# A sliding-window branch beside full attention: V copied into shifted partition groups and summed by a selection matrix, with a new layout table

## The chip, the cores and the metric

The kernel runs on one core of a Trainium2 chip. The metric is the time of one execution on the device in microseconds. Three runs of the kernel before took 825.7, 826.05 and 822.5 us: the median is 825.7.

## The reference

Two attention layers read the same x (2048 tokens, 640 features, 32 heads of 20 features, bf16), and a gate mixes them.

```python
x = A_x
g = sigmoid((x * gate_w).sum(-1, keepdims=True))
a = A_ref(x, A_wqkv, A_wo)      # full softmax attention over 2048 keys
b = B_ref(x, B_wqkv, B_wo)      # 8 taps: key positions s, s-2, ..., s-14
return g * a + (1 - g) * b

# B_ref, after its own q, k, v projections:
W, dil = 8, 2
logits = einsum("bhsd,bhswd->bhsw", q, kg) * Dh ** -0.5   # kg, vg: k, v at the taps
logits = where(mask, logits, -1e9)                        # positions before 0
attn = softmax(logits, axis=-1)
o = einsum("bhsw,bhswd->bhsd", attn, vg)
return o.reshape(B, S, D) @ wo
```

## The kernel before, in words

**Full attention.** The 32 heads form 8 groups of 4, the 2048 queries 4 chunks of 512; a pair of both is one of 32 groups of work, each with 16 key blocks of 128 and 4 heads: 64 blocks of 128 keys x 512 queries. PE computes scores (line 1568, four heads in four row groups of the array), then one of two engines takes the exponential. ACT does most blocks, in tiles of two or three (line 1592, `ebuf`). A block may instead "ride" in the third place of a tile and go to DVE: line 1582 turns the score into a 16-bit integer whose bits are a coarse exponential (`uD`), line 850 makes three shifted copies per four blocks (`eD`), and PE adds four weighted products (line 1637) where a block from ACT needs one. `obank` collects a group; `gen_norm` transposes, divides by the row sums, applies the gate and copies the result into `oTd` by DMA.

**Sliding branch.** It works in 8 units `u` of 256 tokens, with features on partitions in the order 32 * a + head, five chunks f, so a feature is the pair (a, f). `gen_bproj(u)` projects q, k, v into `qkvB` (`qB`, `kB`, `vB`; the last two with 16 columns of the unit before, copied by POOL at line 893). `gen_b(u)` then

1. multiplies q by k shifted, one DVE product of 128x1280 for each of the 8 taps (line 922, into `stage`);
2. sums them over features with the selection matrix `Sel` (line 938): partition 32 * w4 + head then holds the logits of tap w4, with the taps' upper half beside it in the free dimension;
3. takes the maximum over taps on DVE (lines 952 to 960), subtracts it by a matmul (line 964), and lets ACT write `eB` (line 967);
4. copies each tap's 32 rows of `eB` to all four partition groups by four DMAs of 32 KB (`taps`, line 972) into one of three buffers `repB`;
5. computes the row sums and the gate (lines 985 to 1006) and spreads them by DMA into `rB`;
6. multiplies v shifted by the copied tap, again 8 products of 128x1280 (line 1023), once `fold` of the chunk before has freed `oB`;
7. sums the 8 products with identity matmuls (line 610, through `mm_group`): 8 taps for each of three banks, each as four column tiles, and writes `oB` (line 1040).

`gen_fold` multiplies `oB` and `oTd` by the output weights and stores 128 rows at a time. For the last chunk this is done early in part: `gen_prefold` (two row blocks, then, as the third step, the last 128 columns of all four), `gen_prefold2` (the other two row blocks), and `tail` adds what the very last group of heads contributes.

**What sets the order.** All engines run lists in order, with semaphores between them. A planner writes the lists: it goes through the ACT tiles, numbered s, and between them lets generators issue side work on PE and DVE where its own clock says that there is room. Each generator has a priority (the units 5.6, their projections 6.5, prefold 2.2 and so on). `bank` lends one of three PSUM banks (one of its own, the two score tiles' third place). `PLAN` is a table: at certain s it sets 18 knobs, among them how idle DVE must look before blocks ride, how far ahead DVE may be filled, and how full PE must be before filler matmuls (line 1658) are put in. The lines of the change: 50 to 137 (`PLAN`), 489 and 492 (first weights through `repB`), 889 (V's projection waits for the products of the unit before), 914 to 1045 (`gen_b`), 1053 to 1085 (`fold_mms`, `gen_prefold`).

Of the kernel before, what the change touches and what calls it, by code (L numbers as in the profile page):

```python
# [14 lines left out]
P = 128  # L15
# [357 lines left out]
def _build(ctx, nc, A_x, A_wqkv, A_wo, B_wqkv, B_wo, gate_w, out):  # L373
# [16 lines left out]


    NE = 5
    NR = 3
    NV0 = 1
    xT = sb([P, CN, S], BF16, "xT")
    WqP = sb([P, CN, P], BF16, "WqP")
    kvw = sb([P, 3 * CN * D], BF16, "kvw")
    woA_d = sb([P, CN, D], BF16, "woA_d")
    woBp = sb([P, CN, D], BF16, "woBp")
    kT = sb([P, NQ, S], BF16, "kT")  # L400
# [511 lines left out]
    def gen_b(u):  # L912
# [62 lines left out]
        for i in range(NR):  # L975
            taps(i)
# [855 lines left out]
```

## Time and profile before

| | |
|---|---|
| median of three runs | 825.7 us |
| profiled execution, span from first to last instruction | 821.3 us |
| ACT, PE, DVE, POOL busy | 784.6, 771.7, 718.2, 148.0 us |
| ACT tiles of two and of three blocks | 474 and 245 |
| blocks on DVE | 364 |
| products of the sliding branch on DVE | 128, 104.3 us |
| DMA packets | 45014, 29.12 MB |

The profile gives the profiled execution's span and no other time of it; the runs' median stands 4.4 us above the span. PE is an engine for matmuls, PEld its weight loads, DVE the vector engine, ACT the one that does exponentials, POOL a second vector engine, SP the queue that issues nearly all DMAs. In a row of the groups the columns are line, engine, operation, output<-input by the program's names, shapes, count, then busy time in us, mean ns of one, idle time before them and what ended it. In a row of the timeline the columns are start and duration in us, engine, line, operation and count; a row can merge several instructions.

### The profile page before, as it was taken

The page shows a single profiled execution, that of the slowest core. Times are in us where ns is not written, and L with a number is a line of the kernel's source. Part 1 is how long each engine was busy: PE and PEld are TensorE (multiplying, and loading weights), DVE is VectorE, ACT ScalarE, POOL GpSimd, SP SyncE. Part 2 cuts the span into 40 slices and gives each one's busy share as a digit, 9 for nine tenths or more (in the row PEclk, how much of TensorE's full clock was granted, in tenths as well). Part 3 has the DMA queues.
Part 4 walks back from the last instruction along what each step waited for, and adds up shares of the span by engine and source line. Part 5 has one row for each costly group of instructions (what it writes and reads, how often), then busy time and mean ns, then how long its engine had stood idle before and what let it go on. Part 6 is the DMA issues. An engine that isn't in the chain of part 4 may idle for free.

```text
span 821.3 us, 29318 instructions
## 1 busy us (share of the span) xinstructions
PE 771.7 (94%) x12399; PEld 280.8 (34%) x12401; DVE 718.2 (87%) x1261; ACT 784.6 (96%) x752; POOL 148.0 (18%) x204
## 2 busy tenths in 40 slices
PE   8999999989899999999999999999998998989997
PEld 5332223333333332434234332333333323343333
DVE  7587899589998998997899999999899998998973
ACT  4999999999999999999999999999999999999990
POOL 5013114151111111010111021131211121111010
PEclk9999999999999999999999999999999999999999
DMA  9110222100111011011001110010010110110010
GB/s 310 39 36 22 54 45 62 41 15 16 32 31 40 8 43 23 7 44 31 19 6 35 39 37 21 28 32 21 5 30 13 36 21 13 27 33 5 23 41 34
DMA packets 45014, 29.12 MB, mean 35 GB/s; under 512 B 27204, under 2 KB 43684, under 8 KB 44884
## 3 DMA queue, kind: packets, MB, share of 16 engines
q1 hardware_dynamic: 44596, 26.92, 12.6%
q8 instruction: 98, 1.61, 0.8%
q10 hardware_dynamic: 288, 0.33, 0.1%
q14 instruction: 32, 0.26, 0.1%
HBM read 11.94 MB, written 2.62 MB: 18 GB/s over the span
## 4 chain that ended last, share of the span: by engine, by line
PE 37%; ACT 31%; DVE 17%; issue 14%; POOL 0%; ACTq 0%; DVEq 0%
ACT ebuf L1592 30%; PE score L1568 11%; PE obank L1637 9%; PE side L610 9%; DVE uD L1582 7%; DVE eD L850 4%; PE score L610 4%; PE obank L1658 1%; DVE qkvB L906 1%; DVE stage L1023 1%; PE obank L512 1%; DVE stage L922 1%; PE score L1283 1%; ACT eB L967 0%; DVE oB L1040 0%
## 5 line engine op out<-in xcount | busy, mean ns | idle before, releaser
L1592 ACT ACTIVATE ebuf<-score 128x1024 bf16<-128x1024 f32 (+1 forms) x720 | 773.2, 1245 | 9.2 <-PE score L1568 7.7
L1568 PE MATMUL score<-qT,kT 32*128 32x512 bf16 x2048 | 285.0, 385 | 29.2 <-ACT ebuf L1592 18.6
L1582 DVE TENSOR_SCALAR uD<-score 128x512 int16<-128x512 f32 x364 | 240.4, 678 | 20.6 <-PE score L1568 19.3
L850 DVE TENSOR_SCALAR eD<-uD 128x2048 int16<-128x2048 int16 x273 | 192.9, 729 | 2.5 <-PE obank L1637 1.7
L1568 PEld LDWEIGHTS score<-qT,kT 32*128 32x128 bf16 x2048 | 70.8, 91 | 267.4 <-ACT ebuf L1592 186.5
L1637 PE MATMUL obank<-ebuf,vA 128*21 128x512 bf16 x1684 | 156.8, 386 | 1.9 <-DVE eD L850 0.5
L842 POOL TENSOR_TENSOR vS<-vA,vw 128x252 bf16<-128x252 bf16 x91 | 66.7, 735 | 278.6 <-PE obank L1637 246.5
L610 PE MATMUL side<-xT,kvw 128*32 128x256 bf16 (+1 forms) x2550 | 105.9, 282 | 2.4 <-DVE qkvB L906 1.4
L1637 PE MATMUL obank<-eD,vS 128*21 128x512 bf16 x1092 | 95.9, 380 | 0.0
L610 PEld LDWEIGHTS side<-xT,kvw 128*32 128x32 bf16 x2550 | 58.3, 96 | 39.9 <-issue 17.7
L1637 PEld LDWEIGHTS obank<-ebuf,vA 128*21 128x21 bf16 x1684 | 36.9, 89 | 86.1 <-issue 61.4
L817 POOL TENSOR_TENSOR rcp<-rcp,gA 128x16 f32<-128x16 f32 x31 | 9.7, 313 | 306.2 <-DVE rcp L815 306.2
L1023 DVE TENSOR_TENSOR stage<-qkvB,repB 128x1280 bf16<-128x1280 bf16 x64 | 52.7, 844 | 0.1
L922 DVE TENSOR_TENSOR stage<-qkvB 128x1280 bf16<-128x1280 bf16 x64 | 51.6, 834 | 0.1
L906 DVE CAST qkvB<-side 128x512 bf16<-128x512 f32 (+1 forms) x71 | 41.2, 589 | 5.5 <-PE side L610 5.2
L610 PE MATMUL side<-stage,ident 128*32 128x512 bf16 (+1 forms) x704 | 44.7, 348 | 1.0 <-DVE dst L714 0.5
L1637 PE MATMUL obank<-uD,vA 128*21 128x512 bf16 x364 | 35.3, 379 | 0.0
L823 POOL TENSOR_TENSOR oN<-oTt,rcp 128x512 bf16<-128x512 f32 x31 | 33.3, 1074 | 2.4
L1637 PEld LDWEIGHTS obank<-eD,vS 128*21 128x21 bf16 x1092 | 26.8, 92 | 17.2 <-issue 1.4
L811 DVE STREAM_TRANSPOSE oTt<-obank 128x512 f32<-128x512 f32 x32 | 22.7, 709 | 5.2 <-PE obank L1637 4.9
L610 PE MATMUL side<-woA_d,oTd 128*32 128x512 bf16 (+2 forms) x500 | 26.7, 304 | 0.0
L610 PE MATMUL side<-woBp,oB 128*32 128x512 bf16 (+1 forms) x500 | 24.9, 304 | 1.0 <-DVE qkvB L906 0.6
(172 smaller groups left out, 534.9 us busy)
## 6 DMA issues: line engine op xcount, KB each, us to landing
repB<-eB SPq DMA_DIRECT2D x128, 32.0 KB
WqP<-in_A_wqkv_dram SPq DMA_DIRECT2D x16, 160.0 KB
stage<-in_B_wqkv_dram SPq DMA_DIRECT2D x1, 2400.0 KB
oTd<-oN SPq DMA_DIRECT2D x108, 20.0 KB
qT<-dst SPq DMA_DIRECT2D x104, 20.0 KB
out_dram<-outsb SPq DMA_DIRECT2D x12, 160.0 KB
kvw<-in_A_wqkv_dram SPq DMA_DIRECT2D x2, 800.0 KB
oTd<-in_A_x_dram SPq DMA_DIRECT2D x2, 640.0 KB
```

The costliest lines, as they stand in the source:

```text
L610: ins = e.matmul(o[j:k, :], l(j) if callable(l) else l[:, j:k], r, start=(first and i == 0), stop=(last and i == n - 1), skip_group_check= ...
L811: T("dve", 0.625, lambda e: e.transpose(oTt[:, :], obank[:, :]), reads=["obank"], writes=["oTt"])
L823: T(en, c2, lambda e: e.tensor_tensor(oo, ii, ib, ALU.mult), reads=["rcp", "oTt"], writes=["oN0"])
L842: T("pool", 0.607, lambda e: e.tensor_tensor(vS[:, d % 2, :, :], _ap(vA, (kb * NQ + q) * 4 * DV, [[0, K - 1], [1, 4 * DV]]), _ap(vw, 0, [[ ...
L850: T("dve", 0.065 + 0.1334 * n, lambda e, k=k, sl=sl: e.tensor_scalar(eD[:, sl % NS, 0:512 * n].bitcast(I16), uD[d % 2][:, 0:512 * n].bitca ...
L906: t = TB(dvc(n * TOK), lambda e, o=o, i=i: e.tensor_copy(o, i), reads=[("side", b)], writes=[key])
L922: TB(dvc(CN * TOK, 2), lambda e, w=w, ks=ks: e.tensor_tensor(prodB(w), qB[:, :, :], ks, ALU.mult), reads=["qB", "kB"], writes=[("prod", w) ...
L1023: TB(dvc(CN * TOK, 2), lambda e, w=w, vs=vs, rr=rr: e.tensor_tensor(prodB(w), vs, rr, ALU.mult), reads=["vB", ("repB", w4 % NR)], writes=[ ...
L1568: ins = e.matmul(o, kT[32 * j:32 * j + 32, q, kb * P:(kb + 1) * P], qT[g % NQT][32 * j:32 * j + 32, :], start=True, stop=True)
L1582: t = T("dve", 0.598, lambda e: e.tensor_scalar(uD[d % 2][:, 512 * i:512 * (i + 1)].bitcast(I16), side[x], UOFF, 0.0, op0=ALU.add, op1=ALU ...
L1592: exps[s] = T("act", actc(512 * n), lambda e: e.activation(ebuf[s % NE][:, 0:512 * n], score[s % 2][:, 0:512 * n], ACTF.Exp, scale=LN2 / S ...
L1637: ins = e.matmul(obank[32 * j:32 * j + DV, :], v, src, start=(kb == 0), stop=(last and k >= len(lst) - 4), skip_group_check=True)
```

## The change

- **V instead of the taps is copied.** At the end of `gen_bproj(u)`, once the V products of the unit before are done, 16 DMAs fill `vR`, the second part of `stage`: partition group w4 gets all four 32-row groups of `vB`, shifted by 4 * w4 tokens, rows of 258 tokens. The tap copies and `repB` go; V's projection itself no longer waits for the unit before.
- **Taps are numbered anew**: tap w = 2 * w4 + hh. In `vR` partition 32 * w4 + head meets `eB` with the same partition, and the tap sum becomes a sum over partition groups, done by `Sel` with 256 columns (`v_sum`) in place of identity matmuls.
- **Products go by feature chunk**: 5 products of 128x2048 for q and k, 5 for v, in a ring of three buffers, each summed by PE as soon as it is there.
- The maximum gets buffers of its own (`mxB`) and is subtracted by a matmul over 128 rows, with zeros in `negRep` beyond row 32.
- The last chunk of the output weights, 48 rows, is loaded into a zeroed tile (`woA_z`, in the place of `WqP`), so that prefold's matmuls all have 128 rows.
- The first weights go through `ebuf[3]` and `ebuf[4]`.
- `PLAN` has other entries throughout.

```diff
 PLAN = {
-    0: ((0.3, 0.64), 0.31, 1.0, 2.5, 0.49, -1.34, -0.1, 11.8, 7.0, 6.03, 0.52, 0.47, 4.4, 4.0, 0.0, 0.71, 3, -1.5),
...
+    0: ((0.29, 0.69), 0.16, 1.0, 5.5, 0.94, -1.37, 0.17, 9.99, 7.0, 7.54, 0.6, 0.62, 5.69, 5.04, 0.0, 0.65, 2, -3),
...
-    stage = sb([P, WIN * CN * TOK], BF16, "stage")
+    CH = WIN * TOK
+    NCH = 3
+    VW = TOK + DIL
+    stage = sb([P, NCH * CH + 4 * CN * VW], BF16, "stage")
+    vR = _ap(stage, NCH * CH, [[VW, 4 * CN], [1, VW]])
...
-            while m == 2 and u > 0 and not done.get(("bp", u - 1)):
-                yield ("cond",)
...
+        while u > 0 and not done.get(("bp", u - 1)):
+            yield ("cond",)
+        for w4 in range(4):
+            lo = PADB - DIL - 2 * DIL * w4
+            T("sp", 2.0 + 0.65 * 4, lambda e, w4=w4, lo=lo: [e.dma_start(
+                vR[32 * w4:32 * w4 + 32, a * CN:(a + 1) * CN, :], vB[32 * a:32 * a + 32, :, lo:lo + VW]) for a in range(4)],
+              reads=["vB"], writes=[("vR", w4)] + (["stage"] if u == 0 else []), dma=True, nd=4, iss=0.65)
...
+        def q_chunk(f):
+            i = slot[f] = next_chunk()
+            yield ("dve", DVE_AHEAD, sch.free(("prod", i)))
+            o = _ap(stage, i * CH, [[4 * TOK, 2], [TOK, 4], [1, TOK]])
+            i0 = _ap(qkvB, f * TOK, [[0, 2], [0, 4], [1, TOK]])
+            i1 = _ap(qkvB, CN * TOK + f * (TOK + PADB) + PADB, [[-DIL, 2], [-2 * DIL, 4], [1, TOK]])
+            TB(dvc(CH, 2), lambda e: e.tensor_tensor(o, i0, i1, ALU.mult),
...
+        for f in range(NCH):
+            yield from q_chunk(f)
...
+        for f in range(CN):
+            yield from q_sum(f, b)
+            if f + NCH < CN:
+                yield from q_chunk(f + NCH)
...
-        for i in range(NR):
-            taps(i)
...
-        for w4 in range(4):
-            for hh in range(2):
-                w = 4 * hh + w4
-                yield ("dve", DVE_AHEAD, sch.ready(("repB", w4 % NR)))
...
-            if w4 + NR < 4:
-                taps(w4 + NR)
-        done[("bp", u)] = True
+        def v_chunk(f):
+            i = slot[f] = next_chunk()
+            yield ("dve", DVE_AHEAD, max(sch.free(("prod", i)), sch.ready("eB", *[("vR", w4) for w4 in range(4)], to="dve")))
+            o = _ap(stage, i * CH, [[4 * TOK, 2], [TOK, 4], [1, TOK]])
+            i0 = _ap(stage, NCH * CH + f * VW + DIL, [[-DIL, 2], [CN * VW, 4], [1, TOK]])
+            i1 = _ap(eB, 0, [[TOK, 2], [0, 4], [1, TOK]])
...
+        def v_sum(f, k, b):
...
+                    for a in range(4):
+                        ins = e.matmul(side[b][32 * a:32 * a + 32, k * TOK:(k + 1) * TOK], Sel,
+                                       _ap(stage, i * CH + (4 * hh + a) * TOK, [[1, TOK]]),
...
         for f0 in range(0, CN, 2):
             n = min(2, CN - f0)
+            for f in range(f0, f0 + n):
+                yield from v_chunk(f)
...
-            mms = [(side[b][:, 0:n * TOK], ident[:, :], _ap(stage, (w * CN + f0) * TOK, [[1, n * TOK]]))
-                   for w in (0, 4, 1, 5, 2, 6, 3, 7)]
...
+            for k in range(n):
+                yield from v_sum(f0 + k, k, b)
...
-        rows = [P] * (CN - 1) + [D - 4 * DH - (CN - 1) * P]
...
+        wl = [woA_d[:, f, c0:c1] for f in range(CN - 1)] + [woA_z[:, c0:c1]]
...
+    def gen_wz():
+        while not done.get(("q", NG - 1)):
+            yield ("cond",)
+        T("pool", 0.8, lambda e: e.memset(woA_z.bitcast(FP32), 0.0), writes=WQ)
+        rows = D - 4 * DH - (CN - 1) * P
+        T("sp", 5.0, lambda e: e.dma_start(woA_z[0:rows, :], A_wo[D - rows:D, :]), writes=WQ, dma=True)
+        done["wz"] = True
```

More of the change, by code (lines that the diff above doesn't have):

```diff
@@ L444, in _build @@
     rB = sb([P, TOK], FP32, "rB")
[L445 to L447 removed]
+    mxB = [sb([P, TOK], BF16, "mxB%d" % i) for i in range(2)]
+    mB = mxB[1][:, 0:TOK]
+    cB = mxB[0][0:64, 0:TOK]
     oB = sb([P, CN, 512], BF16, "oB")
@@ new lines, in q_sum, with fn @@
+        def q_sum(f, b):
+            rd = [("prod", slot[f]), "Rep"]
+            for hh in range(2):
+                yield ("pe", 0.11, sch.ready(*rd))
+                def fn(e, hh=hh, i=slot[f]):
+                    for w4 in range(4):
+                        ins = e.matmul(side[b][32 * w4:32 * w4 + 32, hh * TOK:(hh + 1) * TOK], Sel,
+                                       _ap(stage, i * CH + (4 * hh + w4) * TOK, [[1, TOK]]),
+                                       start=(hh == 0 and f == 0), stop=(hh == 1 and f == CN - 1), skip_group_check=True)
+                    return ins
+                T("pe", 0.11, fn, reads=rd, mode="col", **({"writes": [("side", b)]} if (hh == 0 and f == 0) else {"accum": [("side", b)]}))
@@ new lines, in v_sum, with fn @@
+        def v_sum(f, k, b):
+            rd = [("prod", slot[f]), "Rep"]
+            for hh in range(2):
+                yield ("pe", 0.11, sch.ready(*rd))
+                def fn(e, hh=hh, i=slot[f]):
+                    for a in range(4):
+                        ins = e.matmul(side[b][32 * a:32 * a + 32, k * TOK:(k + 1) * TOK], Sel,
+                                       _ap(stage, i * CH + (4 * hh + a) * TOK, [[1, TOK]]),
+                                       start=(hh == 0 and k == 0), stop=(hh == 1), skip_group_check=True)
+                    return ins
+                T("pe", 0.11, fn, reads=rd, mode="col", **({"writes": [("side", b)]} if (hh == 0 and k == 0) else {"accum": [("side", b)]}))
@@ L1070, in gen_prefold @@
                 yield ("cond",)
-            rd = [("oTd", (QCN - 1) % 2, q) for q in range(1, NQ)] + ["woA_d", "woBp"] + [
+            rd = [("oTd", (QCN - 1) % 2, q) for q in range(NQ)] + ["woA_d", "woBp"] + WQ + [
                 ("oB", hu, f0) for hu in range(1 + (i == 2)) for f0 in range(0, CN, 2)]
@@ L1096, in gen_prefold2 @@
             yield ("cond",)
-        rd = [("oTd", (QCN - 1) % 2, q) for q in range(1, NQ)] + ["woA_d", "woBp"] + [
+        rd = [("oTd", (QCN - 1) % 2, q) for q in range(NQ)] + ["woA_d", "woBp"] + WQ + [
             ("oB", hu, f0) for hu in range(2) for f0 in range(0, CN, 2)]
```

88 lines of the change are left out of this document (33 added, 55 removed), and 193 rows, old and new, of the table PLAN.

## The prediction

> **What bounds the kernel now.** I read the head of the page first, then the busy time in stretches of 75 us, then the groups of instructions kept apart by shape, and last the order of time at the end.
>
> ```profile
> span 821.3 us, 29318 instructions
> PE 771.7 (94%) x12399; PEld 280.8 (34%) x12401; DVE 718.2 (87%) x1261; ACT 784.6 (96%) x752; POOL 148.0 (18%) x204
> ...
> 325.00:400.00 75.00, 70.22 (x1256) 27.78 (x1248) 66.75 (x118) 74.81 (x71) 10.43 (x19) 1.00 0.09 24
> 475.00:550.00 75.00, 70.84 (x1172) 24.05 (x1164) 71.95 (x126) 74.56 (x74) 15.50 (x20) 1.00 0.12 30
> 800.00:821.30 21.30, 15.44 (x396) 8.01 (x391) 7.70 (x14) 2.39 (x4) 0.00 (x0) 1.00 0.09 33
> ```
>
> The columns of the stretches are PE, PEld, DVE, ACT, POOL, clock, DMA share, GB/s. Inside the run ACT is full: 74.81 of 75 us. DVE has 8.3 us to spare in its emptiest stretch and 3.1 in its fullest. Only at the end ACT is empty: 2.39 of 21.3 us. So time can come from two places: fewer tiles on ACT, which needs DVE to take them, and a shorter end.
>
> ```profile
> L1592 ACT ACTIVATE ebuf<-score 128x1024 bf16<-128x1024 f32 x474 | 458.6, 1099 | 5.5 <-PE score L1568 4.3
> L1592 ACT ACTIVATE ebuf<-score 128x1536 bf16<-128x1536 f32 x245 | 346.8, 1530 | 3.7 <-PE score L1568 3.4
> L1582 DVE TENSOR_SCALAR uD<-score 128x512 int16<-128x512 f32 x364 | 240.4, 678 | 20.6 <-PE score L1568 19.3 <-ACT g L801 0.2
> L850 DVE TENSOR_SCALAR eD<-uD 128x2048 int16<-128x2048 int16 x273 | 192.9, 729 | 2.5 <-PE obank L1637 1.7
> L1023 DVE TENSOR_TENSOR stage<-qkvB,repB 128x1280 bf16<-128x1280 bf16 x64 | 52.7, 844 | 0.1
> L922 DVE TENSOR_TENSOR stage<-qkvB 128x1280 bf16<-128x1280 bf16 x64 | 51.6, 834 | 0.1
> L957 DVE TENSOR_TENSOR repB<-repB 64x256 bf16<-64x256 bf16 x8 | 2.3, 284 | 0.3
> L938 PE MATMUL side<-stage,Rep 128*32 128x256 bf16 x320 | 13.2, 285 | 0.5 <-DVE qkvB L906 0.5
> ...
> L610 PE MATMUL side<-stage,ident 128*32 128x512 bf16 (+1 forms) x704 | 44.7, 348 | 1.0 <-DVE dst L714 0.5
> sum 796.30, PE 34.84 PEld 9.41; mean PE 2.90 PEld 0.78
> ```
>
> The exchange rate: ACT takes (458.6 + 346.8) / (2 x 474 + 3 x 245) = 0.48 us for a head's 128x512 block, DVE (240.4 + 192.9) / 364 = 1.19 us. To end d earlier, ACT must hand over d / 0.48 blocks, so DVE works 2.5 d more in d less time: DVE time freed is worth 1 / 3.5 of itself. The last row is the filler matmuls of line 1658 alone, 34.84 us: PE has that much time without real work, so freeing PE by itself buys little in mid-run.
>
> **The change part by part.** *Products.* 16 of 128x1280 per unit of 256 tokens cost (52.7 + 51.6) / 8 = 13.04 us of DVE. They become 10 of 128x2048. From 284 ns at 256 elements and 834 at 1280 the slope is 0.537 ns, so 2048 take 1.247 us, a unit 12.47, and eight units save 4.5 us. Bounds: in proportion to size 1.334 us each, 2.4 us lost; from the undisturbed pair of the row at 799.44 below (0.775 each) 1.187, 9.4 us saved. I take 4.5, since the slope rests on both sizes; over 3.5 that is **1.3 us** (0.7 lost to 2.7 gained). The Trainium skill (VectorE: DVE Perf Modes, "The perf-mode tier table") gives 1224 ns for such a product of 2048 elements; by it the term would be an estimated 1.8 us instead of 1.3.
>
> *Sums.* The 704 identity matmuls of the row take 44.7 us; the code has 8 x 96 = 768 of them, so in all about 48.8. After, the sum of V works as L938 does for the logits: 320 matmuls of 256 columns, 13.2 us. PE is relieved by 35 us. Most becomes filler or idle. What can count is the 20.6 us in which DVE sat before uD, nearly all for PE's score: at most 20.6 / 3.5 = 5.9 us, at least nothing. I take a quarter, **1.5 us**, nearer to nothing, because the filler time shows that PE is seldom short of time.
>
> *The end.* This is where PE's saving lies on the path.
>
> ```profile
> 784.00 2.28 DVE L1023 TENSOR_TENSOR stage<-qkvB,repB 128x1280 bf16<-128x1280 bf16 x3
> 786.81 2.28 DVE L1023 TENSOR_TENSOR stage<-qkvB,repB 128x1280 bf16<-128x1280 bf16 x3
> 792.07 2.42 SPq L972 DMA_DIRECT2D repB<-eB  x4
> ...
> 796.66 4.64 ACT L1592 ACTIVATE ebuf<-score 128x1536 bf16<-128x1536 f32 x4
> 799.44 1.55 DVE L1023 TENSOR_TENSOR stage<-qkvB,repB 128x1280 bf16<-128x1280 bf16 x2
> 799.89 1.26 PE L1658 MATMUL side<-xT,ident 128*32 128x512 bf16 x20
> 801.79 1.90 PE L610 MATMUL side<-stage,ident 128*32 128x512 bf16 x32
> 804.06 0.45 DVE L825 STREAM_TRANSPOSE oN<-oN 128x256 f32<-128x256 f32 x1
> 806.83 0.46 PE L610 MATMUL score<-woBp,oB 128*32 128x128 bf16 x20 [0.53 <-DVE oB L1040]
> 807.11 0.56 PE L610 MATMUL score<-woA_d,oTd 128*32 128x128 bf16 x20
> 807.61 0.46 PE L610 MATMUL score<-woBp,oB 128*32 128x128 bf16 x20
> 810.76 1.26 PE L610 MATMUL side<-woBp,oB 128*32 128x512 bf16 x20
> 811.85 1.36 PE L610 MATMUL side<-woA_d,oTd 128*32 128x512 bf16 x20
> 812.82 0.10 PEld L610 LDWEIGHTS side<-woA_d,oTd 48*32 48x32 bf16 x4 [0.42 <-issue]
> 813.14 1.26 PE L610 MATMUL score<-woBp,oB 128*32 128x512 bf16 x20
> 815.53 0.41 PE L1116 MATMUL score<-outsb,oN 128*32 128x128 bf16 x16
> ```
>
> ACT's last tile ends at 801.30. The last sliding unit's V products begin at 784.0; six run at once, the last two wait for the fourth tap, which SP fetches at 792.07 into a buffer that the first products had to free, and run at 799.44, ending at 800.99. The sums, their eviction and then the folding of both branches follow: the last unit's sums hold PE from 801.79 to 806.83. After the change the five products need no tap copies; from 784.0, with DVE's other work between, they end by about 792, and the sums with them, before ACT does. What is left behind ACT's end: the last PV (to 802.0); the third prefold, 4 row blocks; the second prefold; the tail. A row block took 0.28 us for B's half and 0.50 for A's (starts 806.83, 807.11, 807.61). A's half is longer since its last chunk has 48 rows and PE stands before it, as the row at 812.82 shows with 0.42 us; with the chunk padded to 128 rows I price both halves alike, 4 x 0.56 = 2.3 us. Each block of the second prefold took 1.09 + 1.29; padded, 2.2, so 4.4. The tail matmuls then start at 802.0 + 2.3 + 4.4 = 808.7 instead of 815.53: **6.8 us**. Late next would be the last group's own transposes, which end at 804.06 + 0.45, so the bound is 815.53 - 804.6 = 10.9 us; at the other side nothing, if the last unit ends as late as now.
>
> *The copies.* 128 copies of 32 KB leave, 128 of 82.5 KB (160 rows of 516 bytes each) come.
>
> ```profile
> 771.31 8.17 SPq L972 DMA_DIRECT2D repB<-eB  x12
> 774.87 0.42 DVE L906 CAST qkvB<-side 128x256 bf16<-128x256 f32 x1 [0.18 <-PE side L610]
> L717 SPq DMA_DIRECT2D qT<-dst x136: 529/718/1773, 60.0 to 687.9; - x136
> q1 hardware_dynamic: 44596, 26.92, 12.6%
> out_dram<-stage ACTq DMA_DIRECT2D x2, 160.0 KB, 1.9
> POOL qkvB L893 <- DVE stage L1023: 35.7, 6, 12.9
> ```
>
> SP issues 16 per unit before (8.17 + 2.42 = 10.6 us) and after: no net cost. They move from behind the exponential to behind the last cast of V. A packet took 0.126 x 821.3 x 16 / 44596 = 37 ns; 16 x 160 per unit are 5.9 us on 16 engines, against some 75 us between units: the DMA share rises from 12.6% to some 17%, and nothing waits for it as long as the copies are early. The halo copy of V on POOL, which stood behind the V products (35.7 us in 6 waits), now stands behind the copies; SP instead waits for the previous unit's products before it overwrites vR, and behind it in SP's order stand q and oTd copies of later groups. I cost both at nothing, because q is made groups ahead.
>
> *Small edits.* The negated maximum as four column tiles of 128 rows, the other mask order, two memsets, first weights through ebuf 3 and 4: start or single instructions, nothing. woA_z is loaded after the last q, whose last copy is issued at 687.9, some 100 us before its use; one memset on a POOL that is 18% busy.
>
> *The table.* It sets how many blocks ride on DVE. In stretches of 75 us line 1582 counts
>
> ```profile
> 100.00:175.00 75.00, 20.52 (x31) 1.00 0.19 45
> 550.00:625.00 75.00, 29.28 (x45) 1.00 0.08 20
> ```
>
> so 14 blocks lie between a poor and a good stretch, 6.7 us of ACT. Over the eight stretches of the sliding branch a shift of half of it either way is 27 us. I take zero, since nothing in the trace shows its sign, and keep the ends for the rivals.
>
> **Sum.** 6.8 + 1.5 + 1.3 = 9.6 us from 821.3, a span of 811.7. The runs shown have a median of 825.7, 4.4 above the profiled span; I leave that distance as it is: **816.1 us**, own range 811 to 821.
>
> **Rivals.** *More blocks ride.* If PE's relief lets all eight stretches fill DVE as the fullest does (71.95; a mean of those two rows is 69.4), DVE gives 8 x 2.6 + 4.5 = 25 us, 7.2 us of time; with the end 14: 811.7. A good table adds a few: 804 to 812. For it: filler time and idle DVE exist. Against: ACT was already fed, so PE was not what held rides back.
>
> *The end does not move.* If the last unit's V products still run after ACT ends, because the fold that frees oB (783 us now) comes later, only 2.8 us remain: 822.9. Against it: the gap from 789 to 799 has no cause but the fourth tap.
>
> *Copies late: slower.* The last V cast of the last unit is at 774.87, its first product at 784.0: 9.1 us. Sixteen issues (10.6) and a landing (1.9, the one that the profile times) need 12.5. If the cast stays so late, a product stands 3.4 us at the head of DVE with uD and eD queued behind, and score tiles behind those. Eight units are 27 us of DVE: 8 us if rides absorb it, 27 if ACT stops with it. At half, 14 us, less 2.8 in mid-run and 4 of the gain at the end: 833. It decides when the casts come less than 12.5 us ahead. Against: the V projection no longer waits for the previous unit's products, so it can be earlier.
>
> *Half clock.*
>
> ```profile
> 690.00:695.00 5.00, 4.49 (x61) 1.56 (x65) 4.18 (x8) 4.18 (x4) 0.00 (x0) 0.66 0.08 20
> ```
>
> Here the clock fell to 0.66 on the mean and ACT stood 0.82 us. PE with 35 us less work could fall more often; twelve more falls cost 9.8 us and give 826, eighteen make it slower. Fillers speak against: 34.84 us of them are there to stop it. [...]
>
> **How the numbers follow.** Forecast 0.45, more rides 0.24, end unmoved 0.13, copies late 0.11, half clock 0.07. A half per cent, 4.1 us, is about what a measurement here tells from no change. Faster takes the first two, 0.05 of the unmoved end and 0.02 of the clock: 0.76; same 0.08 and 0.03: 0.11; slower 0.11 and 0.02: 0.13. The range 805 to 829 leaves out 0.04 of the best tables, 0.11 and 0.02: 0.17.
>
> **What would show it.** Right: the V products of the last unit end before ACT's last tile, the tail matmuls start 7 to 8 us after it (815.53 - 801.30 = 14.2 now), products take near 1.25 us, Sel matmuls double in count at some 26 us, uD counts 365 to 380. Wrong: products with a DMA as releaser, SP copies with long waits for DVE and q late, rows of 0.5 clock in several stretches, fewer than 350 rides, or identity time replaced by waits of PE for the ring of three chunks, which ties DVE and PE together chunk by chunk.

## The result and the profile after

The changed kernel took 818.28 us in the median of 11 runs (813.22 to 822.12), the kernel before 825.04 (821.68 to 826.05) in 11 runs beside it: a ratio of 0.9923, 95% interval 0.9902 to 0.9943. Two later sets of runs on other chips gave 0.9916 (0.9903 to 0.9928) and 0.9899 (0.9877 to 0.9921). So it is faster by 0.8 to 1.0%, some 7 us, against a forecast of 816.1 us in a range of 805 to 829. The profiled execution took 818.97 us, its span is 816.4: 4.9 us shorter than the span before, where the sum of the prediction had 9.6.

First the head of the page, the queue of the copies, three of the stretches that the prediction showed, and the groups kept apart by shape:

```profile
span 816.4 us, 28733 instructions
PE 753.3 (92%) x12136; PEld 276.9 (34%) x12138; DVE 718.1 (88%) x1228; ACT 782.7 (96%) x736; POOL 149.6 (18%) x207
...
q1 hardware_dynamic: 61044, 33.36, 16.7%
```

```profile
325.00:400.00 75.00, 69.94 (x1166) 24.71 (x1158) 69.16 (x120) 74.35 (x71) 14.29 (x21) 1.00 0.10 24
475.00:550.00 75.00, 66.62 (x1112) 24.59 (x1109) 71.38 (x120) 74.23 (x72) 12.39 (x19) 1.00 0.15 35
800.00:816.40 16.40, 11.38 (x324) 6.85 (x314) 7.15 (x12) 5.68 (x7) 0.00 (x0) 0.96 0.12 42
```

```profile
L1634 ACT ACTIVATE ebuf<-score 128x1024 bf16<-128x1024 f32 x435 | 424.8, 1082 | 10.0 <-PE score L1610 8.3
L1634 ACT ACTIVATE ebuf<-score 128x1536 bf16<-128x1536 f32 x269 | 382.6, 1526 | 3.7 <-PE score L1610 3.6
L1624 DVE TENSOR_SCALAR uD<-score 128x512 int16<-128x512 f32 x371 | 244.7, 680 | 24.3 <-PE score L1610 23.6
L1042 DVE TENSOR_TENSOR stage<-stage,eB 128x2048 bf16<-128x2048 bf16 x40 | 49.7, 1255 | 1.0 <-DMA stage<-qkvB 1.0
L945 DVE TENSOR_TENSOR stage<-qkvB 128x2048 bf16<-128x2048 bf16 x40 | 49.6, 1263 | 0.1
L1052 PE MATMUL side<-stage,Rep 128*32 128x256 bf16 x320 | 14.1, 274 | 1.7 <-DVE outsb L1203 0.9 <-DVE qkvB L919 0.7
```

What the change says of its parts is all there: 80 products of 1.26 us on the mean, 320 matmuls more with `Sel` (14.1 us) and no identity sums, DMA share 16.7%, and products that waited for a copy for 1.0 us in the whole run. Blocks on DVE rose from 364 to 371. But ACT, the engine that is full, waited longer for its scores (8.3 + 3.6 us ahead of its two kinds of tiles, 4.3 + 3.4 in the kernel before). Its last tile now ends later, as the order of time at the end shows, with ACT in the first row:

```profile
795.44 9.16 ACT L1634 ACTIVATE ebuf<-score 128x1024 bf16<-128x1024 f32 x8
795.84 2.35 DVE L1042 TENSOR_TENSOR stage<-stage,eB 128x2048 bf16<-128x2048 bf16 x2
800.95 1.22 DVE L1042 TENSOR_TENSOR stage<-stage,eB 128x2048 bf16<-128x2048 bf16 x1
802.22 0.40 PE L1052 MATMUL side<-stage,Rep 128*32 128x256 bf16 x8
802.67 0.42 DVE L1075 SCALAR_TENSOR_TENSOR oB<-side,rB 128x256 bf16<-128x256 f32 x1 [0.51 <-PE side L1052]
803.15 0.46 PE L620 MATMUL score<-woBp,oB 128*32 128x128 bf16 x20
803.72 0.45 PE L620 MATMUL score<-woBp,oB 128*32 128x128 bf16 x20
805.31 0.72 DVE L821 STREAM_TRANSPOSE oTt<-obank 128x512 f32<-128x512 f32 x1 [2.22 <-PE obank L1679]
806.77 1.29 PE L620 MATMUL side<-woBp,oB 128*32 128x512 bf16 x20
808.93 1.29 PE L620 MATMUL score<-woBp,oB 128*32 128x512 bf16 x20
811.09 0.44 PE L1158 MATMUL score<-outsb,oN 128*32 128x128 bf16 x16
```

| | before | after | forecast |
|---|---|---|---|
| ACT's last tile ends | 801.30 | 795.44 + 9.16 = 804.60 | 2.8 earlier |
| row blocks of the third prefold start | 806.83 | 803.15 | |
| tail matmuls start | 815.53 | 811.09 | |
| from ACT's end to the tail matmuls | 14.2 | 6.5 | 7.4 |
| from ACT's end to the end | 20.0 | 11.8 | 13.2 |

So the 4.9 us are a gain of 8.2 behind ACT's last tile and a loss of 3.3 ahead of it. The first came again: two later profiles of the same kernel have 12.2 and 12.0 us from ACT's end to the end. The experiments take the two apart.

### The profile page after: what moved, and what is told of

The parts are those of the page before. It is cut to its first block, busy times and chain, and to the rows that moved or that the text cites. A ratio compares the mean times of both kernels' runs of the same rounds, so it can differ in the third digit from the quotient of the medians.

```text
span 816.4 us, 28733 instructions
## 1 busy us (share of the span) xinstructions
PE 753.3 (92%) x12136; PEld 276.9 (34%) x12138; DVE 718.1 (88%) x1228; ACT 782.7 (96%) x736; POOL 149.6 (18%) x207
## 3 DMA queue, kind: packets, MB, share of 16 engines
q1 hardware_dynamic: 61044, 33.36, 16.7%
## 4 chain that ended last, share of the span: by engine, by line
DVE 30%; PE 26%; ACT 25%; issue 12%; SPq 5%; DMA 1%; POOL 0%; POOLq 0%; ACTq 0%; DVEq 0%
ACT ebuf L1634 24%; DVE uD L1624 11%; DVE eD L860 8%; PE score L1610 7%; PE obank L1679 7%; PE side L620 7%; DVE stage L945 3%; SPq L927 3%; PE score L620 2%; SPq L767 2%; DVE stage L1042 2%; DVE qkvB L919 1%; DVE oTt L821 1%; DMA stage<-qkvB 1%; PE score L1325 1%
## 5 line engine op out<-in xcount | busy, mean ns | idle before, releaser
L1610 PE MATMUL score<-qT,kT 32*128 32x512 bf16 x2048 | 279.4, 386 | 36.0 <-ACT ebuf L1634 20.2
L1624 DVE TENSOR_SCALAR uD<-score 128x512 int16<-128x512 f32 x371 | 244.7, 680 | 24.3 <-PE score L1610 23.6
L860 DVE TENSOR_SCALAR eD<-uD 128x2048 int16<-128x2048 int16 (+1 forms) x279 | 194.8, 719 | 2.3 <-PE obank L1679 1.5
L620 PE MATMUL side<-xT,kvw 128*32 128x256 bf16 (+2 forms) x2720 | 118.1, 287 | 4.9 <-DVE qkvB L919 2.5
L1679 PE MATMUL obank<-eD,vS 128*21 128x512 bf16 x1113 | 99.2, 384 | 0.0
L620 PEld LDWEIGHTS side<-xT,kvw 128*32 128x32 bf16 (+1 forms) x2720 | 62.0, 96 | 49.9 <-issue 19.6
L1042 DVE TENSOR_TENSOR stage<-stage,eB 128x2048 bf16<-128x2048 bf16 x40 | 49.7, 1255 | 1.0 <-DMA stage<-qkvB 1.0
L945 DVE TENSOR_TENSOR stage<-qkvB 128x2048 bf16<-128x2048 bf16 x40 | 49.6, 1263 | 0.1
L620 PE MATMUL side<-woA_d,oTd 128*32 128x512 bf16 (+1 forms) x496 | 25.7, 303 | 0.0
L620 PE MATMUL side<-xT,WqP 128*32 128x512 bf16 x320 | 24.3, 385 | 0.6 <-DVE qkvB L657 0.3
```

The source lines that it names most:

```text
L620: ins = e.matmul(o[j:k, :], l(j) if callable(l) else l[:, j:k], r, start=(first and i == 0), stop=(last and i == n - 1), skip_group_check= ...
L860: T("dve", 0.065 + 0.1334 * n, lambda e, k=k, sl=sl: e.tensor_scalar(eD[:, sl % NS, 0:512 * n].bitcast(I16), uD[d % 2][:, 0:512 * n].bitca ...
L945: TB(dvc(CH, 2), lambda e: e.tensor_tensor(o, i0, i1, ALU.mult), reads=["qB", "kB"], writes=[("prod", i)] + (["stage"] if u == 0 else []), ...
L1042: TB(dvc(CH, 2), lambda e: e.tensor_tensor(o, i0, i1, ALU.mult), reads=["eB"] + [("vR", w4) for w4 in range(4)], writes=[("prod", i)], por ...
L1610: ins = e.matmul(o, kT[32 * j:32 * j + 32, q, kb * P:(kb + 1) * P], qT[g % NQT][32 * j:32 * j + 32, :], start=True, stop=True)
L1624: t = T("dve", 0.598, lambda e: e.tensor_scalar(uD[d % 2][:, 512 * i:512 * (i + 1)].bitcast(I16), side[x], UOFF, 0.0, op0=ALU.add, op1=ALU ...
```

## Experiments

Each ratio is to the kernel before on the same chip. In the table stand median, ratio with its interval, and the granted clock as a mean over all executions of that kernel (for the kernel before it was 0.998 on each of the three later chips).

| kernel | us | ratio | clock |
|---|---|---|---|
| changed kernel, first chip | 818.28 | 0.9923 (0.9902 to 0.9943) | 0.995 |
| changed kernel, second chip | 816.1 | 0.9916 (0.9903 to 0.9928) | 0.998 |
| changed kernel, fourth chip | 816.81 | 0.9899 (0.9877 to 0.9921) | 0.996 |
| nine gaps filled, second chip | 813.47 | 0.9880 (0.9867 to 0.9893) | 0.999 |
| nine gaps filled, fourth chip | 813.19 | 0.9870 (0.9852 to 0.9888) | 0.999 |
| 51 gaps filled, fourth chip | 815.58 | 0.9899 (0.9883 to 0.9915) | 1.000 |
| sums of the last unit four times, second chip | 820.86 | 0.9969 (0.9955 to 0.9983) | 0.996 |
| sums of the other units four times, second chip | 834.64 | 1.0135 (1.0111 to 1.0159) | 0.994 |
| one scaling behind the norm, fourth chip | 822.62 | 0.9987 (0.9971 to 1.0002) | 0.991 |
| without padding, third chip | 818.83 | 0.9941 (0.9920 to 0.9962) | 0.993 |
| before, last unit's sums cut, third chip | 821.88 | 0.9985 (0.9972 to 0.9997) | 0.996 |
| before, the other units' sums cut, third chip | 824.67 | 1.0012 (0.9995 to 1.0029) | 0.990 |
| changed code, table of before, third chip | 848.06 | 1.0299 (1.0274 to 1.0325) | 0.997 |

### The loss ahead of ACT's end: the clock

In the profiled execution after, the clock halved four times in mid-run, at 105, 177, 573 and 781 us; before, once. Busy time in stretches around these places, columns as above (PE first, ACT fourth, then POOL and the clock):

```profile
100.00:105.00 5.00, 3.11 (x39) 1.05 (x43) 4.96 (x11) 5.00 (x5) 0.00 (x0) 1.00 0.36 80
105.00:110.00 5.00, 5.00 (x49) 1.23 (x41) 2.41 (x5) 3.67 (x4) 2.62 (x4) 0.66 0.09 23
...
175.00:185.00 10.00, 8.79 (x93) 2.23 (x89) 8.00 (x12) 8.48 (x9) 4.92 (x4) 0.83 0.09 16
570.00:577.00 7.00, 6.09 (x62) 1.43 (x62) 5.42 (x12) 6.62 (x8) 0.00 (x0) 0.76 0.08 20
778.00:786.00 8.00, 6.37 (x89) 1.96 (x89) 5.59 (x13) 7.82 (x9) 2.20 (x4) 0.79 0.24 68
```

PE did 3.11 us of work in 5, then ran at half clock, full, while ACT lost 1.33 of 5 us; in the next three stretches ACT lost 1.52, 0.38 and 0.18. That is 3.4 us in all. Two of the four lie ahead of the first sliding unit's copies (249.5 us), where none of the identity sums had stood yet, so these two came with the new order and not with the relief of PE. I ran the same program again, and beside it a copy with its gaps filled:

> The changed kernel itself once more, beside the three edits that share its chip, so that they are compared with it and not only with the kernel before. Every theory: 0.990 to 0.994 of the kernel before. The theory of the clock (the TensorE clock halves for 3.4 us at a time after a stretch with gaps on PE, and ACT waits meanwhile) says that the falls come at the same places as in its first profile, about 105, 177, 573 and 781 us, since the order of the work is the same; the rival (falls are chance, and the later end of ACT comes from the new order alone) says that they lie elsewhere in this execution, with ACT's waits for the scores still near 12 us.

> The changed kernel, with one to three groups of four matmuls with zero weights put behind the score matmuls of nine tiles, in the gaps on PE ahead of the four places where the clock fell in the first profile (16 groups, some 0.22 us each; the order of all else is the same). The theory of the clock: at those four places ACT lost 3.4 us (1.33 of 5 us at 104 to 109, 1.52 of 10 at 175 to 185, 0.38 of 7 at 570 to 577, 0.18 of 8 at 778 to 786), so with the falls gone the end comes 2 to 3.4 us earlier, ratio 0.003 to 0.004 below the changed kernel. The rival (the falls only show a stretch where the order already starves PE and ACT, and cost nothing of their own): the clock is whole and the time the same to 0.5 us, or the falls come at another place. A third way: the filling itself delays the scores and the time grows by up to 2 us.

```diff
+    EXTRA = {70: 1, 71: 2, 72: 2, 138: 2, 139: 2, 497: 2, 499: 2, 683: 1, 684: 3}
...
+            for _ in range(extra):
+                for j in range(4):
+                    e.matmul(obank[32 * j:32 * j + 32, :], zero[:, :], xT[:, 0, 0:512], start=False, stop=False,
+                             skip_group_check=True)
```

Tile s issues `extra = EXTRA.get(s, 0)` groups behind its score matmuls: 17 groups (68 matmuls), not the 16 of the expectation.

In the second profile of the unedited kernel the clock fell only once in mid-run (at 569), though PE had the same gap; the order of time gives ACT's end as 783.29 + 18.32 = 801.61:

```profile
100.00:105.00 5.00, 3.28 (x48) 1.16 (x48) 4.55 (x9) 5.00 (x5) 0.81 (x2) 1.00 0.31 65
105.00:110.00 5.00, 4.82 (x67) 1.47 (x63) 4.15 (x7) 5.00 (x5) 2.18 (x3) 1.00 0.09 22
...
783.29 18.32 ACT L1634 ACTIVATE ebuf<-score 128x1536 bf16<-128x1536 f32 x16
```

One program, one order, three falls fewer: ACT ends 3.0 us earlier and the span is 813.8 instead of 816.4. Its one fall cost ACT 0.36 us (6.64 busy of 7 in the stretch 570 to 577). My expectation that falls come at the same places was wrong: which gap brings one differs by execution. It is not the amount of work: the same instructions lie 0.89 us earlier in this profile, and the stretch that matches, 99.11 to 104.11, has 3.10 us of PE work, yet no fall.

What differs is where the gaps lie on a grid of time. In the first profile the falls start at 105.05, 176.73, 572.68 and 780.89 (read from the clock in steps of 0.05 us); the distances are 71.68, 395.95 and 208.21 us, which is 21, 116 and 61 times 3.4133. Take the three profiles of the unedited kernel (the third follows below) between 20 and 808 us in stretches on that grid, each profile's grid laid through its own falls. The clock halved behind all four stretches in which PE worked 2.12 us or less of the 3.41, behind three of the fourteen with 2.18 to 2.34, and behind none with more. The place at 105 had 2.05 us in the first profile, and 2.25 in the second, where the grid lies 0.08 us earlier and the instructions 0.89. PE's busy time is modelled, so these are no exact threshold.

The Trainium skill (TensorE: Matmul & The Clock Gate, Part 1) says that the window over which activity is judged runs freely, and that an idle window brings the half rate. The first agrees with these profiles; the second does not describe these falls, since PE worked 2.05 of the 3.41 us ahead of the fall at 105, and 2.17 ahead of the one at 691 in the kernel before.

With nine gaps filled the time fell by 0.0036 of the time before on that chip, 3.0 us (2.6 by the medians), within what I expected. But its profile also shows one fall (at 488), so the falls alone do not explain it. I therefore repeated it on another chip, with a version that fills far more:

> The changed kernel once more, beside three edits of it. In the runs so far its mean granted clock lay between 0.989 and 1.000 (each fall of 3.4 us takes 0.002 from the mean), and its executions with a clock of 0.997 or more gave 815.8 to 818.9 us. Expected 816 to 819 us here, ratio 0.990 to 0.994; with the mean clock of its executions, it says whether the kernel without padding (mean clock 0.993) was slowed by its edit or by more falls.

> The kernel with 16 groups of zero-weight matmuls in nine gaps, which gave 2.6 us less than the changed kernel on another chip, once more. If what it removes are falls of the clock, its executions again show a higher mean clock than those of the changed kernel beside it, and 2 to 3 us less for 2 to 3 falls (1.0 us for each, by 3.0 us between two profiled executions of the changed kernel, with four falls and with one). The rival (a chance of that chip): the same to 1 us.

> The changed kernel with zero-weight matmuls behind the score matmuls of 51 tiles, one to three groups of four where PE had 0.45 us or more idle before the next scores in the second profile of the changed kernel (up to 77 groups, some 17 us of PE). The theory of the clock: all falls go, the mean clock is 1.000, and the time is 1 to 3 us below the changed kernel, as with nine gaps filled or better. The rival (work given to PE in the middle delays the scores, as the 23 us of repeated sums did, for 18.5 us): slower than the changed kernel, by up to 12 us.

In its third profile the unedited kernel had two falls, at 104 and 490 us (385.7 us apart, 113 times 3.4133); ACT lost 1.46 us in 104 to 109 and 1.55 in 486 to 496, and ended at 790.91 + 13.68 = 804.59. Over the three profiles seven falls cost 6.8 us, 0.2 to 1.5 each.

The gain of the nine filled gaps came again, 0.0029 or 2.4 us (3.6 by the medians). In this profile there is no fall in mid-run; PE works 4.25 of the 5 us at the first place, and ACT ends at 781.45 + 18.28 = 799.73:

```profile
100.00:105.00 5.00, 4.25 (x68) 1.50 (x64) 4.76 (x10) 5.00 (x6) 0.60 (x2) 1.00 0.39 84
105.00:110.00 5.00, 4.82 (x67) 1.34 (x55) 3.94 (x7) 5.00 (x5) 2.38 (x3) 1.00 0.11 26
...
781.45 18.28 ACT L1642 ACTIVATE ebuf<-score 128x1536 bf16<-128x1536 f32 x16
```

With 51 gaps filled (67 groups were issued, by the count of their matmuls) the falls were gone as well (clock 1.000 in the mean, ACT's end 783.23 + 18.28 = 801.51), but the time was 2.4 us above that of nine: filling has a price too. The executions of one kernel bear out the price of a fall: of the kernel before with cut sums (below), those at a mean clock of 0.983 took 827.4 and 827.6 us, those at 0.996 took 821.6 and 822.0. A fall of 3.4 us at half clock takes 1.7 / 820 = 0.0021 from the mean, so these are six falls apart: some 0.9 us for each. Part of the gain of the nine gaps stays unexplained: executions of the changed kernel at clocks of 0.997 or more gave 812.8 to 818.9 us (816.6 in the one at 1.000), those of the filled one 812.1 to 814.1.

### What freed PE time is worth in mid-run

> The kernel before, with the identity sums of the first seven sliding units cut to the first and the last of eight taps (504 matmuls left out, some 25 us of PE between 250 and 780 us; part of the sums is left out, so the output is not the reference's), in the same order of the work. My prediction: 1.5 us for 35 us freed, so about 1.1 us earlier, ratio 0.9987, bounds 0 to 4. The rival that the repeats of the sums suggest (23 us of PE given back to the changed kernel in the middle cost 18.5 us, 0.8 us for each): PE in the middle sets the pace in both orders, and ACT's waits for the scores (7.7 us, of which 3 us at the start) go to 3 us, so 4 to 5 us earlier, ratio 0.994 to 0.995; more isn't to be had, since ACT would then wait for nothing.

```diff
+                    if i in skip:
+                        continue
...
-            yield from mm_group(b, mms, ["ident"] + [("prod", w) for w in range(WIN)], mmc(n * TOK))
+            yield from mm_group(b, mms, ["ident"] + [("prod", w) for w in range(WIN)], mmc(n * TOK),
+                                skip=range(1, 7) if u < 7 else ())
```

> The changed kernel, with the sums of the V products of the first seven sliding units issued four times (three times with zero weights: 840 matmuls of 256 columns, some 23 us of PE between 250 and 775 us, two thirds of what the change frees there); the end is left as it is. My prediction took the relief of PE in the middle for 1.5 us (bounds 0 to 5.9) of 35 us freed: so about 1 us slower, ratio 0.001 above the changed kernel, bounds 0 to 3.9 us. The rival (PE is close to full in the middle and each us there is worth a fifth or more): 5 us slower or more, ratio 0.006 above. If the time stays or falls, the freed PE time was worth nothing in the middle, or its gaps even cost clock.

```diff
+                    for r in range(3 if u < 7 else 0):
+                        for a in range(4):
+                            ins = e.matmul(side[b][32 * a:32 * a + 32, k * TOK:(k + 1) * TOK], zero[:, :],
+                                           _ap(stage, i * CH + (4 * hh + a) * TOK, [[1, TOK]]),
+                                           start=False, stop=(hh == 1 and r == 2), skip_group_check=True)
```

Taking some 25 us of PE out of the kernel before (it leaves those sums out) gained nothing: 1.0012 (0.9995 to 1.0029). Its clock tells why: 0.990 in the mean against 0.998. In its profile, a place where the kernel before had a full PE now has a gap, two falls in a row (6.8 us at half clock from 252.6), and 2.1 of 10 us lost on ACT; first the cut kernel, then the kernel before:

```profile
250.00:260.00 10.00, 9.10 (x78) 2.08 (x78) 5.94 (x10) 7.90 (x9) 1.84 (x3) 0.66 0.10 27
```

```profile
250.00:260.00 10.00, 10.00 (x142) 2.95 (x134) 7.98 (x15) 9.99 (x12) 2.45 (x4) 1.00 0.09 27
```

Where its clock held, it was faster: its five executions at 0.994 to 0.996 took 822.7 us on the mean, the five of the kernel before at 0.995 took 824.7. As far as executions of like mean clock can be compared, the relief was worth some 2 us, and the falls that came with it took them back.

The other way round, 23 us of PE put back into the changed kernel cost 18 us (1.0135 against 0.9916), 14 even in the one execution at full clock (830.26 us against 816.1). ACT's waits in its profile (us in total, times, the longest), against 8.8 us in that of the unedited kernel on that chip:

```profile
ACT ebuf L1639 <- PE score L1615: 30.7, 49, 2.6
```

Both rivals of my term fall: PE time is neither worth a small fraction everywhere nor a price of 0.8. PE runs its list in order, so what is added stands ahead of the next scores at that place, and what is taken leaves a gap that the order does not close, and that can cost clock.

### The gain behind ACT's end

Three edits ask what moved the row blocks from 5.5 us behind ACT's end to 1.5 ahead of it; a fourth asks what the padding is worth.

> The kernel before, with the identity sums of the last sliding unit alone cut to the first and the last of eight taps (24 matmuls of 96 left, some 3.6 us of PE less; six taps are left out, so this part of the output is not the reference's). The theory of the end: in the kernel before these sums stand between ACT's last tile (801.3 us) and the row blocks (806.8 us), so the end comes 2.2 us earlier (if VectorE's three scalings of 0.65, 0.69 and 0.42 us then follow one another) to 3.6 us earlier, ratio 0.9956 to 0.9973. The rival (ACT's last tile and the norm behind it set the end): within 0.5 us of the kernel before.

The sums of the last unit, cut as above for `u == 7`, gained 1.2 us by the ratio (0.9985, 0.9972 to 0.9997) and 1.9 by the medians, less than the 2.2 to 3.6 that I expected. Its order of time at the end, ACT's end being 796.68 + 3.32 = 800.00:

```profile
796.68 3.32 ACT L1595 ACTIVATE ebuf<-score 128x1536 bf16<-128x1536 f32 x3
...
800.92 0.60 PE L612 MATMUL score<-stage,ident 128*32 128x512 bf16 x8
802.73 0.45 DVE L827 STREAM_TRANSPOSE oN<-oN 128x256 f32<-128x256 f32 x1
803.09 0.65 DVE L1043 SCALAR_TENSOR_TENSOR oB<-side,rB 128x512 bf16<-128x512 f32 x1
804.74 0.46 PE L612 MATMUL score<-woBp,oB 128*32 128x128 bf16 x20 [0.53 <-DVE oB L1043]
```

Two of the three sums are done by 801.5, but their scalings stand in VectorE's queue behind the norm of the last A group, whose last transpose starts at 802.73. The row blocks start 4.7 us behind ACT's end instead of 5.5, and ran partly at half clock (0.79 on the mean of 804 to 812 us), behind a wait of PE of 2.28 us. From ACT's end to the end it is 19.8 us, nearly the 20.0 of the kernel before. So the number of matmuls is the small part. The opposite test moves one instruction in the changed kernel (one group of four filler matmuls is gone with it, 260 instead of 264):

> The changed kernel with one instruction moved: the last scaling of the last sliding unit (0.42 us on VectorE) is queued behind the norm of the last A group, as in the kernel before, instead of ahead of it. The theory that the end moved by the place of the scalings in VectorE's queue: the row blocks of the last fold wait for it until the norm is over (about 3.5 us behind ACT's last tile, against 1.45 us ahead of it), of which PE fills 1 us otherwise, so the end comes 3.5 to 4.5 us later, ratio 0.0045 to 0.0055 above the changed kernel; that would be over half of what the end gained. The rival (the end moved since there are fewer sums, wherever the scaling stands): within 1 us.

```diff
             if f0 + 2 >= CN:
                 done[("bs", u)] = True
+            while u == 2 * QCN - 1 and f0 + 2 >= CN and not done.get(("norm", NG - 1)):
+                yield ("cond",)
             yield ("dve",)
             o = oB[:, f0:f0 + n, hu * TOK:(hu + 1) * TOK]
```

The time rose by 0.0088, 7.2 us (by medians 5.8), more than I expected. Its order of time, ACT's end being 797.26 + 6.11 = 803.37, and the stretch of the small row blocks:

```profile
797.26 6.11 ACT L1636 ACTIVATE ebuf<-score 128x1536 bf16<-128x1536 f32 x5
806.47 0.39 DVE L1077 SCALAR_TENSOR_TENSOR oB<-side,rB 128x256 bf16<-128x256 f32 x1
806.91 0.72 PE L620 MATMUL score<-woBp,oB 128*32 128x128 bf16 x20 [2.87 <-DVE oB L1077]
807.95 0.75 PE L620 MATMUL score<-woBp,oB 128*32 128x128 bf16 x20
815.83 0.39 PE L1160 MATMUL score<-outsb,oN 128*32 128x128 bf16 x16
...
804.00:811.00 7.00, 4.13 (x160) 4.09 (x160) 2.63 (x6) 0.00 (x0) 0.00 (x0) 0.57 0.01 2
```

The row blocks start 3.5 us behind ACT's end, just as worked out. What I had not seen: while PE waits 2.87 us the clock halves, and a small row block then takes 1.04 us (806.91 to 807.95) instead of the 0.57 of the changed kernel (803.15 to 803.72), on a path where nothing hides it. From ACT's end to the tail matmuls it is 12.5 us, nearly the 14.2 of before, and to the end 17.7, against 12.0 in the unedited kernel's profile on that chip. The mean clock, 0.991, shows that other falls add to it; three lie in mid-run in this profile.

> The changed kernel, with the sums of the V products of the last sliding unit alone issued four times (three times with zero weights, 120 matmuls of 256 columns, four at a time, some 3.3 us of PE). My theory of the end (the end moved since these sums are few and lie before ACT's last tile, so that PE begins the row blocks of the last fold at 803.2 instead of 806.8): three of the five chunks are summed after 795 us, so about 2 us of the added work fall where PE has less than 1 us idle, and the end comes 1 to 2 us later, ratio 0.001 to 0.0025 above the changed kernel. The rival (the end follows from ACT's last tile and the norm behind it): the same to 0.4 us.

The edit is that of the repeated sums above, for `u == 7`. Here 1.0 to 2.0 us were expected at the end; 4.4 (0.0053) came. In its profile, the fastest of its executions, the span is 2.3 us longer than that of the unedited kernel on that chip, and it is ACT that ends later, at 802.62 + 1.02 = 803.64 instead of 801.61:

```profile
802.62 1.02 ACT L1639 ACTIVATE ebuf<-score 128x1024 bf16<-128x1024 f32 x1 [0.19 <-PE score L1615]
```

At 783 us it was still ahead: its last 16 tiles start at 782.67 instead of 783.29. From ACT's end to the end it takes 12.5 us as against 12.2. So the added sums delayed the scores of the last tiles and left the end alone.

> The changed kernel, with the last input chunk of A's half of the row blocks of the folds at 48 rows again, as before (the order of the work stays). The theory of the padding: the small row blocks of the last fold ahead of the end cost 0.78 us each as before and not 0.56, the two large ones 2.38 and not 2.16; four small and two large blocks lie behind ACT's last tile, so the end comes 1.3 us later, ratio 0.0016 above the changed kernel (0.990 to 0.993 of before). The rival (the norm and its transfers behind ACT's last tile set the start of the last matmuls): the same to 0.3 us.

```diff
-        wl = [woA_d[:, f, c0:c1] for f in range(CN - 1)] + [woA_z[:, c0:c1]]
+        rows = [P] * (CN - 1) + [D - 4 * DH - (CN - 1) * P]
```

The rows are as priced: a small row block takes 0.78 us (804.48 to 805.26), a large one 2.38:

```profile
804.48 0.46 PE L620 MATMUL score<-woBp,oB 128*32 128x128 bf16 x20
805.26 0.46 PE L620 MATMUL score<-woBp,oB 128*32 128x128 bf16 x20
806.41 1.26 PE L620 MATMUL side<-woBp,oB 128*32 128x512 bf16 x20
808.79 1.26 PE L620 MATMUL score<-woBp,oB 128*32 128x512 bf16 x20
```

The time cannot confirm 1.3 us: 0.9941 lies 0.002 to 0.004 above the three ratios of the changed kernel, but with a lower clock (0.993), and its one execution at 0.998 took 815.5 us. The profile shows most of it: ACT ends at 785.36 + 18.20 = 803.56, so it is 12.9 us from there to the end, 0.7 to 1.1 more than in the three profiles of the changed kernel (11.8, 12.2, 12.0).

### Code and table

> The changed code with the layout table of before. The theory that a table fits one code alone (the order that it gives shifts at the first cost that differs, and nothing was weighed for it from there on): 15 to 35 us slower than the changed kernel, above the kernel before, with fewer blocks ridden by VectorE (about 320 of 371) and so more work for ACT. The rival (the code carries the gain and the table is small adjustment): 0.99 to 1.00 of the kernel before.

The changed code with the old table took 848.06 us, 1.0299, and the page shows fewer blocks ridden and more work for ACT:

```profile
L1629 ACT ACTIVATE ebuf<-score 128x1536 bf16<-128x1536 f32 x286 | 400.9, 1518 | 10.0 <-PE score L1605 9.9
L1619 DVE TENSOR_SCALAR uD<-score 128x512 int16<-128x512 f32 x320 | 212.4, 680 | 45.6 <-PE score L1605 44.6
```

The new table is worth some 32 us to this code (1.0299 less 0.9916, times 823.8 us), over four times what the whole change brings. What it would do for the old code was not run.

This run also settles whose gain the end is. With the old table the row blocks start 1.9 us ahead of ACT's end (791.68 + 42.18 = 833.86), and the end comes 11.5 us behind it, at 845.4, as with the new table. The last unit's scaling is over by 799.98 there, long ahead of the norm:

```profile
791.68 42.18 ACT L1629 ACTIVATE ebuf<-score 128x1536 bf16<-128x1536 f32 x35 [0.55 <-PE score L1605]
832.01 0.46 PE L615 MATMUL side<-woBp,oB 128*32 128x128 bf16 x20
```

So the code brings the short end, and the table the mid-run that goes with it.

## Why the prediction was right, and where not

**The end: right in place and nearly in size, half wrong in reason.** Forecast 6.8 us; the tail matmuls start 7.7 us sooner behind ACT's end (14.2 to 6.5), and what follows them is 0.5 us shorter. "The five products need no tap copies; ... they end by about 792" failed: they run at 787.39, 795.84 and 800.95, between other prefold steps, and end at 802.2. "And the sums with them, before ACT does" held, by 2.0 us in this profile and the second. The reason that I gave, fewer sums on PE, is the small part: cutting them in the kernel before moved the row blocks by 0.8 us. What counts is that the products now go by feature chunk, so behind the last product stand one pair of sums and one scaling of 0.42 us, and that this scaling is ahead of the norm in VectorE's queue. Putting it behind took back 5.5 to 6 us of the way from ACT's end to the tail matmuls, 1.9 of them by the clock (four blocks, 0.47 each). The padding is right by its rows (0.56 and 2.16 us a block); of its 1.3 us the profiles show 0.7 to 1.1 and the times nothing sure.

**PE relief, 1.5 us: nothing in the end.** The cut sums of the kernel before gained some 2 us where the clock held, near the forecast, and nothing over all executions. The step that failed is "I take a quarter": it priced waits of DVE before `uD`, which did not shrink (20.6 before; 24.3, 21.4 and 22.9 in the three profiles after), and it left out what the relief costs in clock. PE's busy time fell by 18 to 23 us in these profiles, not by 35.

**Products, 1.3 us: the size was right, the exchange is not shown.** Forecast 1.247 us each, measured 1.255 and 1.263. The sum set a mean duration against a busy time; by busy time alone a unit went from 13.04 to (49.7 + 49.6) / 8 = 12.41 us, so 5.0 us were saved instead of 4.5. The 1224 ns that the Trainium skill gives (VectorE: DVE Perf Modes, "The perf-mode tier table") lie 3% under the means and fit the medians (1217 ns in both rows). The seven blocks more on DVE cover 7 x 0.48 = 3.4 us of ACT by the prediction's rate, but ACT's end does not show them. Without what the falls cost, it comes at 801.2, 801.3 and 801.6 in the three profiles after and at 800.5 before (801.30 less 0.82): 0.7 to 1.1 later, against a forecast of 2.8 earlier. With nine gaps filled and no fall it comes at 799.73, with 51 filled at 801.51. Why mid-run gave nothing stays open beyond that.

**Half clock: the term that was missing.** I had it as a rival with a chance of 0.07, at 0.82 us a fall and twelve falls, and as nothing in the sum. A fall costs about 1 us, as priced; but the changed kernel has more of them: by its mean clocks (0.995, 0.998, 0.996 against 0.998) not quite one more on the mean, and three more in the profiled execution, so that a sign that I had named for being wrong, half clock in several stretches, did come. Somewhat under 1 us belonged into the sum. In the profiled execution the falls cost 2.6 us more than before (3.4 against 0.82); with the two terms above, which gave nothing, that makes up most of why ACT's end came 3.3 us late where 2.8 early was forecast. In the second profile, with one fall as before, it came 0.3 late.

**Where luck helped.** The gain at the end was 1.4 larger than forecast and covered part of what mid-run did not give. And the time came nearer (818.28 against 816.1) than the span (816.4 against 811.7), since the 4.4 us that I carried over between span and median were 1.9 here. The size of the total is in part two errors of opposite sign.

**Copies, small edits.** Copies cost next to nothing: DVE waited 0.7 to 2.0 us for them in the three profiles, the DMA share is 16.7% as worked out (some 17%). The rival of late copies is refuted.

**The table.** "I take zero" came out right only for code and table together, which is luck: with the old table the new code is 24 us slower than the kernel before (848.06 against 823.77), more than the sum of its parts can say, and the new table takes some 32 us from that.

**Rivals.** More blocks ride: 7 more, not the 15 and more that it needed. The end does not move: refuted. The forecast of faster at 0.76 was borne out.

## What to carry to other kernels

Freed time on an engine that runs a list in order may be worth little by itself (some 2 us for 25 here, and nothing once falls of the clock came with it): ask what the next instruction on the full engine waits for, and whether the gap left behind costs clock. At the end of a kernel, look at the queue of the engine that does the last small step: one scaling of 0.42 us behind another branch's norm cost 5.8 us here. And when work is taken from TensorE, count the falls of the clock over several executions; a few matmuls with zero weights in the worst gaps gave the fastest version of all, 813.2 us.

## What the runs showed that I had not expected

- The clock halves for some 3.4 us without an idle stretch of that length, and its falls start on a grid of 3.413 us: the same gaps (3.11 and 3.10 us of work in 5) brought a fall in one execution and none in another, as they lay on the grid.
- A fall costs ACT 0.2 to 1.5 us in mid-run, and on a path that TensorE alone sets far more: the small row blocks took 1.04 us instead of 0.57.
- Identity sums that looked like waste kept the clock up: without most of them the mean granted clock went from 0.998 to 0.990, and the 2 us gained by the relief were gone.
